# Reordered row loads, transposes and a weight load ahead of the first batch's last transform

## The chip, the cores and the metric

The kernel runs on one core of one Trainium2 chip. The metric is the device time of one execution in microseconds (us). Engines are named as in the profile: PE (TensorE, matmuls and transposes), DVE (VectorE), ACT (ScalarE), POOL (GpSimd) and SP (SyncE, which here only issues DMAs). DMAs issued by SP go through one queue (q1, hardware descriptors), DMAs issued by POOL through another (q0, software descriptors).

## The reference

The input `x` is 8 batches of 3136 rows by 256 channels, float32. Per batch and channel the rows are Fourier transformed, multiplied by a complex filter and transformed back; then a low-rank mix over the rows is added, and a two-layer perceptron over the channels.

```python
X = np.fft.rfft(x, axis=1)
Y = X * (filt_r + 1j * filt_i)
y = np.fft.irfft(Y, n=3136, axis=1)
u = y + (y^T @ U @ V)^T              # U: 3136x32, V: 32x3136
out = u + relu(u @ w_ch1) @ w_ch2    # w_ch1: 256x1024, w_ch2: 1024x256
```

## The kernel before

The 3136-point transform is split as 49 x 64. For one batch there are these stages, each a Python generator from which a hand-written order takes steps.

- `f1` / `f1_turned` (L241, L265): the 49-point transforms, a matmul with the table `ws` over four chunks `c` of `x`. `load_x` (L124) brings a chunk from float32 in DRAM to f16 in SBUF on POOL's queue.
- `mid` (L312): 64-point transform (`pz`, L374), product with the filter on DVE (`uv`, L382), inverse 64-point transform (`pe`, L338), copied by ACT to `e` (L348). There are 13 steps: pairs of frequencies, and the frequency 0 in a step of its own (the third, for batch 0). For batches 0 and 1 the input is turned on PE by `turn` (L289) instead of going through DRAM.
- The results are rearranged through DRAM. Every second pair is **stored** from `e` to `ct2` (L356, SP, 256 KB; batch 0 has five such stores, here store 1 to 5), and **row loads** (`load_e2`, L402, DMA at L406, SP) bring them to `eb`, in which partitions 32 to 95 hold the 48 frequencies' parts and the free dimension 64 rows of 256 channels. `load_e2(b, part, hs)` loads part 0, 1 or 2 (from stores 1-2, 3-4, 5) for row half 0, half 1 or both. In batch 0 the last two pairs go straight from `e` to `eb` without DRAM, by four small DMAs on SP and four on POOL (L352, 32 KB each).
- `rank` (L409): the low-rank part. `uh`, the transformed U, is multiplied with `e`; the result goes to `eb[0:32]` (L428, DVE).
- `s4` (L435): the last transform. Sixteen tiles `pu` of eight matmuls each (L446); the first eight need row half 0 of `eb`, the other eight row half 1. Batch 0 adds a matmul of constants to each tile (L443). DVE (L453) and ACT (L451) copy the tiles to `ut`.
- Then the main loop over 49 groups of 512 rows: `mm1` with `w1sb` (`phh`, L478, and ReLU on ACT, L481) and `mm2` with `w2sb` (`pc`, L501, L493, copied by DVE, L508). `plan` deals the steps of the later batches among the groups.

Ahead of the main loop everything of batch 0 runs in the order written from L532 on. Instructions of one engine run in program order, and a DMA that has to wait for an earlier one holds up all that its issuing engine has after it. PSUM tiles come from three tags of banks: `z` with 4, `m` and `o` with 2 each.

U is transformed first (`u_hat`, L210) into `tu`, which lies in `eb`. `u_ordered` (L224) copies part of it to `tp`, and `u_turned` (L227) makes 29 transposes on PE into two `z` banks and three copies on ACT to `uh`. `load_filters(i)` (L151, POOL's queue) loads the filters in three parts, and `spread_filters(i)` (L159) copies each part to partitions 64 to 127; for part 2 these are four copies on POOL. `w1sb` is loaded after them on POOL's queue (L538); `v_rows` (L201) is the POOL copy after that.

On POOL, `seen` (L563, L565) is a copy of a few elements of `eb`, which makes POOL wait until certain row loads have landed before it issues `load_x(1, 1)`, `load_x(1, 2)`, `load_x(1, 3)` and the load of `w2sb`.

Of the kernel before, what the change touches and what calls it, by code (L numbers as in the profile page):

```python
# [17 lines left out]
NK = 25  # L18
DM = 256
RANK = 32  # L20
# [59 lines left out]
def kernel(  # L80
# [37 lines left out]
    def view(t, off, dims):  # L118
        return bass.AP(tensor=t.tensor, offset=t.offset + off, ap=[[t.ap[0][0], t.shape[0]]] + [list(d) for d in dims])
# [39 lines left out]
    def spread_filters(i):  # L159
        s = slice(PARTS[i], PARTS[i + 1])  # L160
        copies = ((nc.vector.tensor_copy, nc.vector.tensor_copy), (nc.vector.tensor_copy, nc.scalar.copy),
                  (nc.gpsimd.tensor_copy, nc.gpsimd.tensor_copy))[i]

        for s in (slice(PARTS[2], 19), slice(19, NK)) if i == 2 else (s,):
            for f, copy in enumerate(copies):
                copy(fab[64:128, f, s, :], fab[0:64, f, s, :])


    a20 = [cst.tile([128, DM], F16, name=f"a20_{i}") for i in range(2)]
# [3 lines left out]
    uh = cst.tile([128, NK + 4, RANK], F16)  # L173
    nc.gpsimd.memset(uh[64:128, 0, :], 0)

    for i in range(3):
        load_filters(i)

    vnat = sb.tile([RANK, SEQ], F16, tag="ut", bufs=2, name="vnat")
    nc.gpsimd.dma_start(vnat, moe_V)  # L180
    w1sb = cst.tile([128, 2, NH], F16)
    w2sb = cst.tile([128, 8, DM], F16)

# [38 lines left out]
    tp = cst.tile([RANK, 4, 128], F16)  # L222

    def u_ordered():  # L224
        nc.scalar.copy(view(tp, 0, [[64, 8], [32, 2], [8, 4], [1, 8]]), view(tu, 128 * 20, [[64, 8], [8, 2], [16, 4], [1, 8]]))

    def u_turned():  # L227
        pt = bank("z", "put", F16)
        for k in range(NK):
            src = tu[:, 128 * k - 128:128 * k] if k else tu0  # L230
            m = 128 if k else NR
            nc.tensor.transpose(pt[0:m, RANK * k:RANK * k + RANK], src, idn[0:RANK, 0:RANK])
        pd = bank("z", "pd", F16)
        for k in range(4):
            nc.tensor.transpose(pd[:, RANK * k:RANK * k + RANK], tp[:, k, :], idn[0:RANK, 0:RANK])
        nc.scalar.copy(uh[:, 1:NK, :].rearrange("r k u -> r (k u)"), pt[:, RANK:RANK * NK])
        nc.scalar.copy(uh[0:NR, 0, :], pt[0:NR, 0:RANK])
        nc.scalar.copy(uh[:, NK:, :].rearrange("r k u -> r (k u)"), pd[:, 0:4 * RANK])


    def f1(b):  # L241
# [47 lines left out]
    def turn(b, g):  # L289
        if g == 3:  # L290
            t = a20[b]
            pt = bank("z", "pt", F16)
            for dh in range(2):
                nc.tensor.transpose(pt[0:64, 128 * dh:128 * dh + 128], t1[b][1][:, dh, :], idn)
            nc.scalar.copy(t[0:64], pt[0:64, 0:DM])
            return t
        t = sb.tile([128, 8, DM], F16, tag="a2", bufs=3, name="a2")
        for half in range(2):
            pt = bank("z" if b else ("m", "z")[half], "pt", F16)
            for i in range(4):  # L300
                for dh in range(2):
                    nc.tensor.transpose(pt[:, 256 * i + 128 * dh:256 * i + 128 * dh + 128],
                                        t1[b][0][:, dh, 8 * g + 4 * half + i, :], idn)
            (nc.scalar.copy if half or (g and b == 0) else nc.vector.tensor_copy)(  # L304
                t[:, 4 * half:4 * half + 4, :].rearrange("p k d -> p (k d)"), pt)
        return t
# [5 lines left out]
    def mid(b, tag="z"):  # L312
        a2 = {}

        def load_a2(g):
            if b < 2:
                a2[g] = turn(b, g)
                return
            if g == 3:
                t = a20[b % 2]  # L320
                nc.sync.dma_start(t[0:64], ct0[b].ap())
            else:
                t = sb.tile([128, 8, DM], F16, tag="a2", bufs=3, name="a2")
                nc.sync.dma_start(t, dram(ct1[b], 8 * g * DM, [[24 * DM, 128], [1, 8 * DM]]))
            a2[g] = t

        def s3(ks, uv, o):
            n = len(ks) * DM
            i = (ks[0] - 1) // 2
            pe = bank(tag, "pe")  # L330

            direct = b == 0 and ks[0] > 20
            ms = (gmp, gsmp) if direct or not ks[0] else (gm, gsm)
            if b == 0 and ks[0] > 8:

                nc.tensor.matmul(pe, m64[:, 0:128], m64[:, 0:512], start=True, stop=True, skip_group_check=True)
            for f, w in enumerate(ms if b == 0 else ms[:1]):
                nc.tensor.matmul(pe[:, 0:n], w, uv[:, f, o:o + n], start=(f == 0), stop=(b > 0 or f == 1))  # L338
            if not ks[0]:
                e3[b, 6] = sb.tile([128, DM], F16, tag="e30", bufs=2, name="e30")  # L340
                nc.scalar.copy(e3[b, 6], pe[:, 0:n])

                nc.sync.dma_start(eb[96:97, :, :], e3[b, 6][0:64])
                return
            if i % 2 == 0:
                e3[b, i // 2] = sb.tile([128, 4, DM], F16, tag="e3", bufs=6, name="e3")
            t = e3[b, i // 2]
            nc.scalar.copy(t[:, 2 * (i % 2):2 * (i % 2) + 2, :].rearrange("p k d -> p (k d)"), pe)  # L348
            if direct:
                for n, k in enumerate(ks):  # L350
                    for part in range(2):
                        (nc.sync if part else nc.gpsimd).dma_start(  # L352
                            eb[32 + row_of(k, part):33 + row_of(k, part), :, :],
                            t[64 * part:64 * part + 64, 2 * (i % 2) + n, :])
            elif i % 2:
                nc.sync.dma_start(dram(ct2[b][i // 4], 2 * (i % 4 - 1) * 128 * DM, [[DM, 128], [128 * DM, 4], [1, DM]]), t)  # L356

        if b == 0:
            spread_filters(0)
        for g in (0, 3, 1, 2) if b > 1 else (0, 3):  # L360
            load_a2(g)
        todo = []
        first_at = 2 if b < 2 else 6
        for i, ks in enumerate(PAIRS[:first_at] + [(0,)] + PAIRS[first_at:]):
            n = len(ks) * DM
            if b == 0 and i == 1:
                spread_filters(1)
            if b < 2 and i in (3, 7):
                load_a2(i // 4 + 1)
            pz = bank("z", "pz")  # L370
            if ks[0]:
                src = a2[(ks[0] - 1) // 8]
                k = (ks[0] - 1) % 8
                nc.tensor.matmul(pz, a2m, src[:, k:k + 2, :].rearrange("p k d -> p (k d)"), start=True, stop=True)  # L374
            else:
                nc.tensor.matmul(pz[:, 0:n], a20m, a2[3], start=True, stop=True)
            o = 512 if ks[0] % 4 == 3 else 0
            if o == 0:
                uv = sb.tile([128, 2, 1024], F16, tag="uv", bufs=4, name="uv")
            zin = bass.AP(tensor=pz.tensor, offset=pz.offset, ap=[[pz.ap[0][0], 128], [0, 2], [1, n]])  # L380
            fin = view(fab[:, 0, ks[0], 0:1], 0, [[NK * DM, 2], [1, n]])
            nc.vector.tensor_mul(uv[:, :, o:o + n], zin, fin)  # L382
            todo.append((ks, uv, o))
            if b and (o or not ks[0]):

                nc.vector.tensor_sub(uv[0:64, 0, 0:o + n], uv[0:64, 0, 0:o + n], uv[64:128, 1, 0:o + n])  # L386
                nc.vector.tensor_add(uv[64:128, 0, 0:o + n], uv[64:128, 0, 0:o + n], uv[0:64, 1, 0:o + n])  # L387
            if len(todo) > (3 if b else 2):
                s3(*todo.pop(0))
            yield  # L390
        for n, it in enumerate(todo):
            s3(*it)
            if b or n == 0:
                yield
        if b == 0:
            load_e2(0, 2, [0])
            load_e2(0, 1, [1])
            load_e2(0, 2, [1])
        yield


# [128 lines left out]
    s4s = [s4(b) for b in range(NB)]  # L530

    u_hat()  # L532
    for _ in f1s[0]:
        pass
    nc.gpsimd.dma_start(sv[32:97], sv_d.rearrange("k (r q) -> k r q", q=NQ))
    load_x(1, 0)
    spread_filters(2)
    nc.gpsimd.dma_start(w1sb, moe_w_ch1.rearrange("(h dd) c -> dd h c", h=2))  # L538
    v_rows(nc.gpsimd.tensor_copy, 0, 32)
    for i in range(13):  # L540
        next(mids[0])
        if i == 7:
            u_ordered()
        if i == 8:
            load_e2(0, 0)
            u_turned()
    load_e2(0, 1, [0])
    next(mids[0])
    next(ranks[0])
# [10 lines left out]
            next(f1s[1])  # L560
        nc.tensor.matmul(pw, m64[:, 0:128], m64[:, 0:512], start=(i == 0), stop=(i == 6))

    nc.gpsimd.tensor_copy(seen[64:66], eb[64:66, 8, 0:4])  # L563
    load_x(1, 1)
    nc.gpsimd.tensor_copy(seen[64:96], eb[64:96, 40, 0:4])  # L565
    for c in range(2, 4):
        load_x(1, c)
    nc.gpsimd.dma_start(w2sb, moe_w_ch2.rearrange("(t cc) e -> cc t e", t=8))
    for _ in s4s[0]:
        pass  # L570
# [60 lines left out]
```

## Time and profile before

| | us |
|---|---|
| runs of the kernel (3): median | 523.7 |
| lowest, highest | 521.31, 523.73 |
| profiled execution, its time | 523.45 |
| profiled execution, span of its instructions | 521.7 |
| PE busy | 497.5 (95% of the span) |
| ACT / DVE / POOL busy | 376.2 / 352.8 / 81.7 |
| mean granted PE clock | 0.984 |

The span runs from the first to the last instruction; times inside it are counted from its start. The page cuts the span into 40 slices of 13 us and gives, for each, the busy tenths of every engine and the granted PE clock in tenths of full speed. Other views list the instructions in order of time, the chain of waits that ended last, the busy time in chosen stretches, and the DMA queues in a stretch.

### The profile page before, as it was taken

The page shows a single profiled execution, that of the slowest core. Times are in us where ns is not written, and L with a number is a line of the kernel's source. Part 1 is how long each engine was busy: PE and PEld are TensorE (multiplying, and loading weights), DVE is VectorE, ACT ScalarE, POOL GpSimd, SP SyncE. Part 2 cuts the span into 40 slices and gives each one's busy share as a digit, 9 for nine tenths or more (in the row PEclk, how much of TensorE's full clock was granted, in tenths as well). Part 3 has the DMA queues.
Part 4 walks back from the last instruction along what each step waited for, and adds up shares of the span by engine and source line. Part 5 has one row for each costly group of instructions (what it writes and reads, how often), then busy time and mean ns, then how long its engine had stood idle before and what let it go on. Part 6 is the DMA issues. An engine that isn't in the chain of part 4 may idle for free.

```text
span 521.7 us, 11949 instructions
## 1 busy us (share of the span) xinstructions
PE 497.5 (95%) x4841; PEld 357.0 (68%) x4841; DVE 352.8 (68%) x470; ACT 376.2 (72%) x705; POOL 81.7 (16%) x121
## 2 busy tenths in 40 slices
PE   4794999999999999999999999999999999999997
PEld 4443666776777777777767777777677766776665
DVE  5885599589847987579747985689845995622122
ACT  6672778966996689767986689667985777666662
POOL 6672010002001111002101120002001010101110
PEclk9896799999999999999999999999999999999999
DMA  8995916966878297837877397828875136212213
GB/s 194 173 229 124 176 39 154 283 218 149 208 222 265 66 186 198 292 137 163 219 230 249 70 189 217 286 99 191 233 232 204 62 127 200 100 44 83 80 41 122
DMA packets 67287, 88.09 MB, mean 169 GB/s; under 512 B 4875, under 2 KB 51787, under 8 KB 67232
## 3 DMA queue, kind: packets, MB, share of 16 engines
q0 software_dynamic: 14768, 41.65, 32.6%
q1 hardware_dynamic: 52464, 45.68, 28.9%
q8 instruction: 38, 0.62, 0.5%
q14 instruction: 17, 0.14, 0.1%
HBM read 55.07 MB, written 47.64 MB: 197 GB/s over the span
## 4 chain that ended last, share of the span: by engine, by line
PE 85%; DVE 3%; DMA 1%; ACT 1%; SPq 1%; issue 0%
PE pc L501 32%; PE phh L478 32%; PE pu L446 5%; PE pc L493 4%; PE pf L250 4%; PE pe L338 3%; PE pz L374 3%; DVE uv L382 2%; DMA eb<-ct 1%; PE ph L413 1%; ACT h L481 0%; DVE uv L386 0%; DVE uv L387 0%; DVE och L508 0%; SPq L352 0%; DVE a L304 0%
## 5 line engine op out<-in xcount | busy, mean ns | idle before, releaser
L481 ACT ACTIVATE h<-phh 128x512 f16<-128x512 f32 x392 | 236.5, 605 | 87.7 <-PE phh L478 86.6
L478 PE MATMUL phh<-ut,w1sb 128*128 128x512 f16 (+7 forms) x896 | 234.3, 353 | 0.4 <-DVE ut L453 0.2
L501 PE MATMUL pc<-w2sb,h 128*128 128x256 f16 x1568 | 234.2, 272 | 0.0
L501 PEld LDWEIGHTS <-h 128*128 128x128 f16 x1568 | 151.5, 97 | 90.4
L508 DVE COPY och<-pc 128x512 f32<-128x512 f32 x98 | 67.6, 690 | 99.6 <-PE pc L493 98.4
L382 DVE TENSOR_TENSOR uv<-pz,fab 128x1024 f16<-128x1024 f32 (+1 forms) x104 | 120.9, 1179 | 13.4 <-PE pz L374 11.9
L513 POOL DMA_DIRECT2D out_dram<-och x48 | 39.1, 814 | 402.7 <-DVE och L508 395.1
L478 PEld LDWEIGHTS <-w1sb 128*128 128x128 f16 x896 | 77.9, 98 | 19.7 <-issue 2.2
L348 ACT CAST e<-pe 128x512 f16<-128x512 f32 x96 | 56.7, 591 | 19.3 <-PE pe L338 18.4
L453 DVE CAST ut<-pu 128x392 f16<-128x392 f32 x92 | 48.9, 559 | 24.6 <-PE pu L446 21.0
L255 ACT CAST asb<-pf 98x512 f16<-98x512 f32 x96 | 57.3, 600 | 0.2
L493 PE MATMUL pc<-idn,ut 128*128 128x128 f16 (+1 forms) x400 | 54.0, 219 | 0.0
L446 PE MATMUL pu<-sv,eb 97*128 97x49 f16 x1024 | 41.9, 189 | 6.8 <-DMA eb<-ct 6.8
L428 DVE COPY eb<-h 32x4096 f16<-32x4096 f16 x32 | 38.2, 1232 | 14.2 <-ACT h L425 14.2
L446 PEld LDWEIGHTS <-eb 97*128 97x128 f16 x1024 | 38.9, 99 | 8.0 <-issue 7.2
L338 PE MATMUL pe<-uv,m 128*128 128x512 f16 (+1 forms) x117 | 41.3, 371 | 2.0 <-ACT e L348 1.0
L493 PEld LDWEIGHTS <-ut 128*128 128x128 f16 (+1 forms) x400 | 38.2, 98 | 5.2 <-issue 0.8
L374 PE MATMUL pz<-a,m 128*128 128x512 f16 x96 | 36.6, 384 | 1.4 <-DVE a L304 1.0
L250 PE MATMUL pf<-x,ws 98*98 98x256 f16 x192 | 36.6, 273 | 0.0
L386 DVE TENSOR_TENSOR uv<-uv 64x1024 f16<-64x1024 f16 (+1 forms) x49 | 30.9, 630 | 1.7
L387 DVE TENSOR_TENSOR uv<-uv 64x1024 f16<-64x1024 f16 (+1 forms) x49 | 30.7, 627 | 0.7
L250 PEld LDWEIGHTS <-ws 98*98 98x98 f16 x192 | 22.4, 125 | 9.1 <-issue 0.4
(81 smaller groups left out, 226.2 us busy)
## 6 DMA issues: line engine op xcount, KB each, us to landing
out_dram<-och POOLq DMA_DIRECT2D x48, 512.0 KB, 3.9
ct<-e SPq DMA_DIRECT2D x47, 256.0 KB
eb<-ct SPq DMA_DIRECT2D x46, 256.0 KB
x<-in_x_dram POOLq DMA_DIRECT2D x28, 392.0 KB, 6.7
ct<-asb SPq DMA_DIRECT2D x24, 384.0 KB
a<-ct SPq DMA_DIRECT2D x18, 512.0 KB
x<-in_x_dram POOLq DMA_DIRECT2D x4, 384.0 KB, 8.0
ws<-ws SPq DMA_DIRECT2D x1, 600.2 KB
```

Source lines behind the costliest of these rows:

```text
L250: nc.tensor.matmul(pf[0:98, 256 * s:256 * s + 256], ws[:, (8 * c + j) * 98:(8 * c + j + 1) * 98], t[:, j, :], start=(s == 0), stop=True, s ...
L255: nc.scalar.copy(dst, src)
L338: nc.tensor.matmul(pe[:, 0:n], w, uv[:, f, o:o + n], start=(f == 0), stop=(b > 0 or f == 1))
L348: nc.scalar.copy(t[:, 2 * (i % 2):2 * (i % 2) + 2, :].rearrange("p k d -> p (k d)"), pe)
L374: nc.tensor.matmul(pz, a2m, src[:, k:k + 2, :].rearrange("p k d -> p (k d)"), start=True, stop=True)
L382: nc.vector.tensor_mul(uv[:, :, o:o + n], zin, fin)
L446: nc.tensor.matmul(pu[:, NQ * i:NQ * i + NQ], eb[:, 8 * n + i, d], sv[:, 8 * g + i, :], start=(i == 0), stop=True, skip_group_check=True)
L478: nc.tensor.matmul(ph[:, o:o + n], w1sb[:, dh, 128 * t:128 * t + 128], utv(b)[:, dh, t0:t0 + n], start=(dh == 0), stop=(dh == 1), skip_gro ...
L481: nc.scalar.activation(h, ph, RELU)
L493: nc.tensor.matmul(d, w, idn, start=False, stop=(dh == 1), skip_group_check=True)
L501: nc.tensor.matmul(o, gr.h[tt][:, 128 * i:128 * i + 128], w2sb[:, tt, :], start=(tt == 0), stop=False, skip_group_check=True)
L508: nc.vector.tensor_copy(gr.och[:, i - 1:i + 1, :], gr.pc.rearrange("p (j d) -> p j d", d=DM))
```

## The change

Six edits, all ahead of the main loop.

1. `load_filters(1)`, `load_filters(2)` and the load of `vnat` stand after `u_hat()` in the program, and `u_ordered()` is put ahead of them, as a POOL copy instead of an ACT copy.
2. The 29 transposes of U stand ahead of the steps of `x`'s last chunk in `f1_turned(0)`, in one bank of tag `m` instead of two of tag `z`; the copies to `uh` stay after step 8 of `mid` (steps are counted from 0) and are two instead of three.
3. In `turn`, batch 0's tiles take other tags of banks.
4. The load of `w1sb` stands between the two pairs of POOL copies of filter part 2 instead of after both.
5. Part 0's row loads: before, both halves were issued after step 8 (after store 3, ahead of store 4). Now half 0 is issued after step 10 (after store 4), and half 1 together with half 1 of parts 1 and 2, after all loads of half 0.
6. `seen` copies from partitions 32 to 63 and 64 to 95, of half 0 ahead of `load_x(1, 1)` and of half 1 ahead of `load_x(1, 2)`; before, ahead of `load_x(1, 1)` it read two partitions alone.

```diff
     def spread_filters(i):
...
             for f, copy in enumerate(copies):
                 copy(fab[64:128, f, s, :], fab[0:64, f, s, :])
+            yield
...
-    for i in range(3):
-        load_filters(i)
+    load_filters(0)
     vnat = sb.tile([RANK, SEQ], F16, tag="ut", bufs=2, name="vnat")
-    nc.gpsimd.dma_start(vnat, moe_V)
...
     def u_ordered():
-        nc.scalar.copy(view(tp, ...), view(tu, 128 * 20, ...))
+        nc.gpsimd.tensor_copy(view(tp, ...), view(tu, 128 * 20, ...))
     def u_turned():
-        pt = bank("z", "put", F16)
+        pt = bank("m", "put", F16)
...
-        pd = bank("z", "pd", F16)
         for k in range(4):
-            nc.tensor.transpose(pd[:, RANK * k:RANK * k + RANK], tp[:, k, :], idn[0:RANK, 0:RANK])
-        nc.scalar.copy(uh[:, 1:NK, :]..., pt[:, RANK:RANK * NK])
+            nc.tensor.transpose(pt[:, RANK * (NK + k):RANK * (NK + k + 1)], tp[:, k, :], idn[0:RANK, 0:RANK])
+        return pt
+    def u_copied(pt):
+        nc.scalar.copy(uh[:, 1:, :]..., pt[:, RANK:RANK * (NK + 4)])
         nc.scalar.copy(uh[0:NR, 0, :], pt[0:NR, 0:RANK])
-        nc.scalar.copy(uh[:, NK:, :]..., pd[:, 0:4 * RANK])
...
     def turn(b, g):
-            pt = bank("z", "pt", F16)
+            pt = bank("z" if b else "o", "pt", F16)
...
-            pt = bank("z" if b else ("m", "z")[half], "pt", F16)
+            pt = bank("m" if b == 0 and g == 1 and half == 0 else "z", "pt", F16)
...
         if b == 0:
             load_e2(0, 2, [0])
-            load_e2(0, 1, [1])
-            load_e2(0, 2, [1])
+            for part in range(3):
+                load_e2(0, part, [1])
...
     u_hat()
-    for _ in f1s[0]:
-        pass
+    u_ordered()
+    for i in range(1, 3):
+        load_filters(i)
+    nc.gpsimd.dma_start(vnat, moe_V)
+    for i in range(16):
+        if i == 12:
+            put = u_turned()
+        next(f1s[0])
     nc.gpsimd.dma_start(sv[32:97], ...)
     load_x(1, 0)
-    spread_filters(2)
+    late = spread_filters(2)
+    next(late)
     nc.gpsimd.dma_start(w1sb, ...)
+    next(late)
     v_rows(nc.gpsimd.tensor_copy, 0, 32)
     for i in range(13):
         next(mids[0])
-        if i == 7:
-            u_ordered()
         if i == 8:
-            load_e2(0, 0)
-            u_turned()
+            u_copied(put)
+        if i == 10:
+            load_e2(0, 0, [0])
     load_e2(0, 1, [0])
...
-    nc.gpsimd.tensor_copy(seen[64:66], eb[64:66, 8, 0:4])
-    load_x(1, 1)
-    nc.gpsimd.tensor_copy(seen[64:96], eb[64:96, 40, 0:4])
-    for c in range(2, 4):
-        load_x(1, c)
+    for h in range(2):
+        for p in (32, 64):
+            nc.gpsimd.tensor_copy(seen[p:p + 32], eb[p:p + 32, 8 + 32 * h, 0:4])
+        for c in ((1,), (2, 3))[h]:
+            load_x(1, c)
     nc.gpsimd.dma_start(w2sb, ...)
```

## The prediction

> **What bounds it now.** I read the page first: PE is busy 95% of the span, and the low digits stand in the first five slices alone, with the granted clock low in the fourth and fifth (39 to 65 us). All six edits lie there. Behind it PE is the bound; a main loop that starts earlier ends earlier by the same time.
>
> ```profile
> PE   4794999999999999999999999999999999999997
> ...
> PEclk9896799999999999999999999999999999999999
> ```
>
> Then I took the chain of waits from 36 to 60 us and the instructions of SP and of PE in order of time (columns: start, length, what).
>
> ```profile
> 42.37 0.59 SPq L352
> ...
> 43.90 0.58 SPq L406
> 44.48 0.04 issue
> 44.52 6.65 DMA eb<-ct
> 51.17 0.14 issue
> 51.30 0.49 PE pu L446 x8
> ```
>
> ```profile
> 27.91 3.63 SPq L356 DMA_DIRECT2D ct<-e  x2
> 31.91 1.22 SPq L406 DMA_DIRECT2D eb<-ct  x2
> 33.47 2.09 SPq L356 DMA_DIRECT2D ct<-e  x2
> 39.89 0.52 SPq L406 DMA_DIRECT2D eb<-ct  x1
> 40.50 2.46 SPq L352 DMA_DIRECT2D eb<-e  x4
> 43.06 2.15 SPq L406 DMA_DIRECT2D eb<-ct  x3
> ```
>
> ```profile
> 46.59 0.49 PE L446 MATMUL pu<-sv,eb 97*128 97x49 f16 x8 [5.68 <-DMA eb<-ct]
> ...
> 51.30 0.49 PE L446 MATMUL pu<-sv,eb 97*128 97x49 f16 x8 [1.09 <-DMA eb<-ct]
> ```
>
> The reader is to see two waits of PE for row loads: 5.68 us ahead of half 0, 1.09 us ahead of half 1. SP issues stores 2 and 3 at 27.91 and 31.18, stores 4 and 5 at 33.47 and 35.20, and then sits until 39.89: part 1's load waits for store 4, which the trace's semaphore records have landing at 39.87, 6.4 us after its issue (store 3: 6.7). Behind that wait stand the four direct DMAs and the last loads. From store 4's landing to the first `pu` are 6.7 us: 0.57 for the load's issue, 2.56 for four direct DMAs, 3.0 from the issue of part 2's half 0 at 43.06 to its landing at 46.07, and 0.5 until PE runs.
>
> Why does a store take 6.4 us? Two stretches of the DMA view (queue: packets, MB, share of the engines' time):
>
> ```profile
> q0 software_dynamic: 202, 0.41, 91.5%
> ```
>
> ```profile
> q1 hardware_dynamic: 1513, 1.20, 103.8%
> q0 software_dynamic: 19, 0.02, 3.7%
> ```
>
> The first is 31.5 to 34.5 us, the second 35.0 to 38.5. In the first, `w1sb` (POOL's queue, issued at 29.97) moves 0.41 MB and SP's queue has no packet at all, although two stores and two loads are issued by then. When `w1sb` is through, SP's queue moves 1.20 MB in 3.5 us (343 GB/s): stores 3, 4, 5 and the two early loads, in that order.
>
> **The change part by part.**
>
> *`w1sb` earlier (edit 4).* It goes ahead of two POOL copies of 1.46 us: issued at about 27.1 instead of 29.97. POOL's queue is then still busy with a chunk of `x`, whose packets end near 29, so `w1sb` runs from about 28.9 to 32.6 (0.51 MB at 0.41 MB per 3.0 us). The price: stores 1 and 2 (25.99, 27.91), which before used the gap from 28.5 to 31, now stand behind it. The two copies end 0.74 us later (its issue), near 30.8; the first product that needs them is the eleventh, not before 31.9. That cover is 1 us; were it gone, DVE would wait the difference.
>
> *U's transposes earlier (edits 1 to 3).* At 29.81 PE spends 1.11 us on them between steps of `mid` (29.81 to 30.92). Now they run while PE waits for the last chunk (14.46 to 15.54, 1.07 us): cost 0 to 0.1. DVE's products are back to back from 21.95 to 28.3 and from 28.46 to 30.8, then wait 0.53 for `pz` behind the transposes; that goes, the last product ends 0.5 earlier. ACT loses `u_ordered` (0.6, just ahead of store 3's second copy) and one copy of U (0.25, against 0.1 for the longer first one): store 3 goes 0.5 earlier, store 4 0.95, to about 32.5, store 5 0.8. What is late next is ACT's chain of `e`, the U copies still in it. `u_ordered` as a POOL copy has no row; bounds are 0.5 (512 elements at the 1.46 us per 1536 of L166) and 1.0 (at the 2.91 us per 1568 of the strided L202). I take 1.0: it starts near 12.5, where POOL waits until 13.31 anyway, and the filter loads behind it wait for `x` again at 15.54, which absorbs the rest. The banks: `put` holds one `m` bank from 14.5 to step 8; in that time `m` serves the last chunk's second tile and one tile of `turn`, whose bank ACT or DVE has emptied by 17.3. Cost 0.
>
> *Half 0 first (edit 5).* Ahead of store 4 in SP's queue now stand no loads. In order after `w1sb` (32.6): store 1, the DMA of frequency 0, stores 2, 3, 4: 1.08 MB at 343 GB/s is 3.1 us, so store 4's packets end at 35.7. Before, they ended near 38.1 by the same reckoning (35.0 and four transfers of 0.262 MB), 15 of its 16 parts landed at 38.68 and the last at 39.87; a tail of 0.6 to 1.8, of which I take 1.1: landing 36.8 (bounds: 34.8, with the 2.3 us of the quiet store at 84.42; 38.9, with the old 6.4). Half 0 of part 0 needs stores 1 and 2 and can hold SP to about 35, not beyond store 4's landing. Then the same 6.7 us: **first `pu` at 43.5 instead of 46.59, 3.1 us earlier** (bounds 41.5 and 45.6).
>
> *Half 1 and the chunks of `x` (edits 5, 6).* SP issues half 1's three loads right behind, to about 42.5; at 3.0 to 4.4 us to landing (the rows at 43.06 and 43.90) they are in by 47. PE needs 3.5 us for half 0, to 47.0. `load_x(1, 1)` now waits for all of half 0: landing 43.0 and 1.0 us as between 48.31 and 49.35, issue 44.0 (before 44.17), packets 2.3 us later (before: 44.17 to 46.5), at 46.3, so it no longer holds up half 1, whose last load took 6.65 us before. The wait of 1.1 goes. Chunks 2, 3 and `w2sb` follow half 1's landing: about 48 instead of 49.35; chunk 3 then lands near 55, needed near 55.6, and `w2sb` near 58 (8.9 us after its issue before), needed near 58.4. That cover is thin, and half a microsecond late would cost as much.
>
> *Clock.* Granted clock by windows (columns: window, its length, PE, PEld, DVE, ACT and POOL busy, PEclk, DMA share, GB/s):
>
> ```profile
> 13.40:16.80 3.40, 1.96 (x38) 1.65 (x35) 2.42 (x9) 2.22 (x10) 2.28 (x5) 1.00 1.15 172
> 16.80:20.20 3.40, 3.23 (x20) 1.94 (x20) 2.42 (x6) 1.28 (x4) 3.37 (x6) 0.50 1.00 138
> ...
> 50.90:54.30 3.40, 3.00 (x64) 3.03 (x65) 1.70 (x3) 1.27 (x3) 0.98 (x2) 0.50 0.81 150
> 54.30:57.70 3.40, 3.18 (x25) 1.79 (x22) 0.66 (x2) 2.02 (x5) 0.00 (x0) 0.50 1.21 184
> ```
>
> The clock changes at steps of 3.41 us in the trace's clock records. PE idle for 1.4 of 3.4 us halves it in the next step; it stays 0.50 to 57.76, since the wait at 50.2 breaks the dense stretch. After the change `pu` runs without a gap, so one dense step fits and the clock returns near 48 to 50. A tile takes 0.43 at half clock; at full clock DVE's 0.57 for every second tile sets 0.29. Some four tiles gain 0.14 each, and the first ReLU comes 0.4 earlier (four `phh` take 1.87 where 0.43 per pair is the later rate): 1.0 us (bounds 0 and 2.4).
>
> **Sum.** 3.1 + 1.1 + 1.0 = 5.2 us off the profiled execution's 523.45 (span 521.7 and 1.75 around it): **518.3**. The profiled time stands 0.25 under the median, so nothing is corrected for that.
>
> [...]
>
> **Rivals.**
> - *The wait moves to stores 1 and 2.* Held behind `w1sb`, they land late, SP stands at half 0 of part 0, and store 5 and all behind it follow. For it: no store got through beside `w1sb`. Against: the queue needs only 1.6 us for both once `w1sb` is through. If SP stood there until 37, part 2's half 0 would end the wait, `pu` would start near 45.2: 1.4 earlier, with the 1.1 of half 1 and no clock, 521.0. Chance 0.14.
> - *Slower: half 1 falls behind `load_x(1, 1)`.* If SP reaches half 1's three loads after the chunk's packets start (over 4 us later than I put it), 0.64 MB wait for the chunk's 4 us of packets: in by 52, `pu` ends near 55.5 instead of 54.8, and chunk 3 and `w2sb`, now behind half 1, come 3 us late. That is 1 to 3 slower: 525.5. For it: the load issued at 44.52 landed at 51.17. Against: half 0's landing now gates the chunk. Chance 0.06.
> - *The clock does not fall.* The idle stretch shrinks to some 3 us over two steps. Then the tiles run at 0.29 from the start, 2.4 us less for sixteen, and the main loop starts 0.5 faster: 3.1 + 1.1 + 2.9 = 7.1, 516.3. Chance 0.08, as the row at 13.40 speaks against it.
>
> **Numbers.** My forecast has 0.72. The range reaches from 516.2, just under the clock rival, to 521.8, over the first rival, and leaves the slower one and the ends of the unknown tail out. About 0.5%, 2.6 us, is what can be told from no change: faster than 521.1 holds my forecast, the clock rival and a small part of the first: 0.81; within it 0.13; slower 0.06.
>
> **What would show it.** SP: store 4 at 32.5, landing before 38; the direct DMAs from about 37.4. PE: first `pu` between 42 and 45, no wait of 1 us ahead of the ninth tile. q0 with packets from 29 to 32.6, then q1 alone. PEclk back at 1.00 before 51. First `phh` near 50 instead of 55.05. Wrong: store 4 landing after 39, a new wait of SP ahead of part 0's load that lasts beyond 36, PE waiting for chunk 3 or `w2sb`, or DVE for the filter copies near 32.

## The result, and the profile after

| | before | changed |
|---|---|---|
| median of 9 runs each, us | 523.6 (519.62 to 523.73) | 518.92 (517.33 to 521.4) |
| ratio to before, with 95% interval | 1 | 0.9932 (0.9903 to 0.9961) |
| profiled execution, us | 523.45 | 517.65 |
| its span, us | 521.7 | 515.9 |
| first `pu`, ninth `pu`, first `phh`, first `pc` | 46.59, 51.30, 55.05, 63.05 | 43.90, 46.50, 49.94, 57.24 |

The change is faster by 0.7% by the ratio, which here is that of the means (519.05 to 522.60); the medians differ by 4.7 us, or 0.9%. A time of 518.3 was forecast. Line numbers of `seen` and of the loads at the end of POOL's list differ by some ten between the two kernels; those of the rows below are the same.

The page of the changed kernel, the two rows shown of before:

```profile
PE   4787999999999999999999999999999999999997
...
PEclk9898999999999999999999999999999999999999
```

PE's fourth slice has gone from 4 to 7 tenths, and the granted clock of the fourth and fifth from 6 and 7 to 8 and 9. (In the third, PE has gone from 9 to 8.) The instructions of SP in order of time (start, length, what):

```profile
27.95 5.03 SPq L356 DMA_DIRECT2D ct<-e  x3
35.58 0.59 SPq L406 DMA_DIRECT2D eb<-ct  x1
36.27 0.53 SPq L356 DMA_DIRECT2D ct<-e  x1
37.08 0.53 SPq L406 DMA_DIRECT2D eb<-ct  x1
37.66 2.52 SPq L352 DMA_DIRECT2D eb<-e  x4
40.23 3.23 SPq L406 DMA_DIRECT2D eb<-ct  x4
```

Stores 2, 3 and 4 leave at 27.95, 30.76 and 32.62. Then SP stands until 35.58 for part 0's load, since store 2 lands at 35.49 by the semaphore records (31.82 before: `w1sb`, which lands at 35.00, is now in its way). Store 5 waits behind it, from the end of its copy near 34.7 to 36.27. Store 4 lands at 37.00, 2.9 us sooner than before, and the rest follows. PE, with what ended its waits:

```profile
43.90 0.36 PE L446 MATMUL pu<-sv,eb 97*128 97x49 f16 x8 [3.27 <-DMA eb<-ct]
...
54.54 0.35 PE L278 MATMUL pf<-ws,x 98*128 98x98 f16 x4 [0.17 <-DMA x<-in_x_dram]
...
57.24 0.60 PE L501 MATMUL pc<-w2sb,h 128*128 128x256 f16 x4 [0.23 <-DMA w2sb<-in_moe_w_ch_dram]
```

The 5.68 us ahead of half 0 are 3.27; the wait ahead of half 1 is gone. Two new short waits stand where the cover was said to be thin, for chunk 3 and for `w2sb`, and the chain of waits now runs through `w2sb`'s load:

```profile
37.08 5.67 DMA eb<-ct
42.77 3.48 DMA eb<-ct
...
48.41 8.79 DMA w2sb<-in_moe_w_ch_dram
57.20 0.04 issue
57.24 0.60 PE pc L501 x4
```

The clock, by windows (columns as in the prediction; PEclk is the third from the end):

```profile
45.20:48.60 3.40, 3.40 (x77) 3.40 (x73) 2.71 (x6) 2.05 (x5) 1.62 (x5) 0.50 0.84 141
48.60:52.00 3.40, 3.01 (x54) 2.20 (x51) 1.73 (x4) 2.67 (x8) 1.26 (x2) 1.00 0.91 155
```

One step at half clock instead of four. **What makes the time:** from the first `pc` to the end of the span are 458.65 us before (521.7 - 63.05) and 458.66 after (515.9 - 57.24), and 458.6 to 458.7 in all but two of the experiments below (458.9 and 459.3 there). All that this change can move lies ahead of the first `pc`, so the start of `pc` in a profile stands for its time. The same kernel spreads by some 4 us from run to run (more in some of the experiments), and two profiles of the changed kernel have the first `pc` at 57.24 and 59.51, so single profiles are read for mechanisms and the ratios for sizes.

### The profile page after: what moved, and what is told of

It is laid out like the page before. It is cut to its first block, busy times and chain, and to the rows that moved or that the text cites. A ratio compares the mean times of both kernels' runs of the same rounds, so it can differ in the third digit from the quotient of the medians.

```text
span 515.9 us, 11950 instructions
## 1 busy us (share of the span) xinstructions
PE 494.3 (96%) x4841; PEld 354.1 (69%) x4841; DVE 352.3 (68%) x470; ACT 375.0 (73%) x703; POOL 82.4 (16%) x124
## 4 chain that ended last, share of the span: by engine, by line
PE 86%; DMA 7%; DVE 4%; ACT 2%; issue 1%; POOL 0%; POOLq 0%; SPq 0%
PE pc L501 32%; PE phh L478 31%; PE pu L446 5%; PE pf L250 4%; PE pc L493 4%; PE pe L338 4%; PE pz L374 4%; DMA eb<-ct 2%; DVE uv L382 2%; DMA w2sb<-in_moe_w_ch_dram 2%; DMA x<-in_x_dram 2%; DMA usb<-in_moe_U_dram 1%; PE ph L413 1%; DMA ct<-e 1%; ACT a L304 1%; ACT e L348 1%
## 5 line engine op out<-in xcount | busy, mean ns | idle before, releaser
L453 DVE CAST ut<-pu 128x392 f16<-128x392 f32 x92 | 48.6, 559 | 20.0 <-PE pu L446 18.6
L446 PE MATMUL pu<-sv,eb 97*128 97x49 f16 x1024 | 40.5, 187 | 3.3 <-DMA eb<-ct 3.3
L446 PEld LDWEIGHTS <-eb 97*128 97x128 f16 x1024 | 37.6, 98 | 4.4 <-DVE eb L428 3.6
```

The source lines that it names most:

```text
L446: nc.tensor.matmul(pu[:, NQ * i:NQ * i + NQ], eb[:, 8 * n + i, d], sv[:, 8 * g + i, :], start=(i == 0), stop=True, skip_group_check=True)
```

## The experiments

Ratios are to the kernel before on the same chip, with 95% intervals; "changed" has 0.9932 (0.9903 to 0.9961).

| kernel | median us | ratio | first `pu`, first `pc` in its profile |
|---|---|---|---|
| changed, again | 518.93 | 0.9933 (0.9909 to 0.9957) | 45.31, 59.51 |
| changed without edit 4 | 519.27 | 0.9932 (0.9902 to 0.9961) | 45.54, 59.08 |
| changed without edit 5 | 521.98 | 0.9989 (0.9953 to 1.0025) | 48.35, 62.38 |
| changed without edit 6 | 519.8 | 0.9941 (0.9907 to 0.9974) | 43.41, 58.23 |
| changed without edits 1 to 3 | 518.82 | 0.9928 (0.9899 to 0.9958) | 46.33, 64.37 (a late execution) |
| before with edit 5 | 522.15 | 1.0021 (0.9995 to 1.0047) | 44.64, 61.06 |
| before with edits 5 and 6 | 520.39 | 0.9963 (0.9946 to 0.9981) | 45.29, 60.95 |
| changed, `w1sb` away | 518.91 (one run) | | 41.20, 58.51 |
| changed, PE kept busy | 520.29 | 0.998 (0.996 to 1.0001) | 43.57, 58.24 |
| changed, `sv` late | 518.86 | 0.995 (0.9933 to 0.9968) | 44.86, 58.83 |
| changed, `sv` on SP | 519.42 | 0.995 (0.9928 to 0.9971) | 45.56, 60.84 |
| changed, chunk 1 early, PE kept busy | 520.52 | 0.9965 (0.994 to 0.9989) | 46.12, 59.07 |

### One edit taken back at a time

**Edit 4**, `w1sb` behind the four copies again:

```diff
     next(late)
-    nc.gpsimd.dma_start(w1sb, ...)
     next(late)
+    nc.gpsimd.dma_start(w1sb, ...)
```

> The changed kernel with the load of w1sb put back behind all four filter copies. My theory (software-queue transfers shut out SP's queue, so w1sb's place decides which stores are late): w1sb's packets run 31.5 to 35.0 us again, stores 1 and 2 land by 32 as before, stores 3 and 4 wait for w1sb; store 4 lands at 37.2 to 38.4 instead of 37.0 and the first pu starts at 44.0 to 45.1 instead of 43.9: 0.1 to 1.2 us longer. Rival A (w1sb's place is the gain): first pu at 46, some 2.5 us longer. Rival B (queues share the engines, its place does not matter): stores 3 and 4 land as in the changed kernel, first pu at 43.9.

Measured: `w1sb` issued at 30.05, stores 1 and 2 in at 30.91 and 31.77, stores 3 and 4 at 36.52 and 37.28. Store 4 lands 0.3 us later than in the changed kernel, and the ratio is the same to the last digit. What `w1sb` shuts out on one side of store 2 it lets through on the other. Its first `pu`, at 45.54, is later than I expected, but the changed kernel's other profile has 45.31. Rival A is refuted; rival B, for the total, can't be told from my theory by this run.

**Edit 5**, both halves of part 0 ahead of store 4 again:

```diff
         if i == 8:
+            load_e2(0, 0)
             u_copied(put)
-        if i == 10:
-            load_e2(0, 0, [0])
```

> The changed kernel with part 0's row loads, both halves, back after step 8, ahead of store 4. My theory: with w1sb early, store 2 lands only at 35.5, SP stands at part 0's loads until then, so store 4 is issued near 36.8 instead of 32.6 and lands near 40; the first pu starts at 46.5 to 47.5 and the kernel is 2 to 4 us slower than the changed one, no better than the kernel before. Rival A (edits 4 and 6 are worth their gain without edit 5): first pu at 44.5, under 1 us slower than the changed one.

SP in order of time:

```profile
26.94 3.17 SPq L356 DMA_DIRECT2D ct<-e  x2
35.05 1.22 SPq L406 DMA_DIRECT2D eb<-ct  x2
36.37 1.08 SPq L356 DMA_DIRECT2D ct<-e  x2
41.73 0.52 SPq L406 DMA_DIRECT2D eb<-ct  x1
```

Store 2 lands at 34.96, part 0's loads wait for it, and store 4, whose data were ready long before, leaves at 36.37 and lands at 41.72. The first `pu` starts at 48.35, and the gain over the kernel before is within its interval of nothing. That is my theory; but store 4 landed 1.7 us later than I put it, and the first `pu` came 0.9 us after the end of my range.

**Edit 6**, the old `seen`:

```diff
-    for h in range(2):
-        for p in (32, 64):
-            nc.gpsimd.tensor_copy(seen[p:p + 32], eb[p:p + 32, 8 + 32 * h, 0:4])
-        for c in ((1,), (2, 3))[h]:
-            load_x(1, c)
+    nc.gpsimd.tensor_copy(seen[64:66], eb[64:66, 8, 0:4])
+    load_x(1, 1)
+    nc.gpsimd.tensor_copy(seen[64:96], eb[64:96, 40, 0:4])
+    for c in range(2, 4):
+        load_x(1, c)
```

> The changed kernel with the old seen copies, so that load_x(1,1) waits for two partitions of half 0 only. My theory: it is issued near 43.2 instead of 44.25, its packets start near 44.5, and the last of half 1's rows are shut out until they are through: they land near 48 to 50 instead of 46.24, PE waits 1 to 3 us ahead of the ninth pu, and the kernel is 0.5 to 2.5 us slower. Rival (half 1's rows are through by then, or the queues share): they land by 46.5, no wait, and chunks 2, 3 and w2sb come 1 us sooner, so 0 to 0.4 us faster.

My theory did not come true. The chunk left at 42.82, half 1's last load at 42.23 landed at 46.76, and PE did not wait for it (ninth `pu` at 46.90). The rival's picture holds: with SP as early as this, half 1 is ahead of the chunk without the new `seen`. The ratio is inside the changed kernel's interval. Only `w2sb` did not come sooner (58.19).

**Edits 1 to 3**, U as before (the place of the filter loads, which is part of edit 1, stays as in the changed kernel):

```diff
-    u_ordered()
     for i in range(1, 3):
...
-        if i == 12:
-            put = u_turned()
...
+        if i == 7:
+            u_ordered()
         if i == 8:
-            u_copied(put)
+            u_turned()
```

> The changed kernel without edits 1 to 3: U ordered on ACT and turned at step 8 in two z banks. My theory: store 4 is issued near 33.5 instead of 32.6, DVE's last product ends 0.5 later, and since store 2's landing (35.5) and not store 4's issue holds SP here, the first pu starts only 0 to 0.9 us later: 0 to 0.9 us slower. Rival (the transposes are the larger part of the gain): first pu 2 us later, 2 us slower.

0.9928: nothing lost, the low end of what I expected; the rival's 2 us are refuted by the ratio. Its profiled execution is the slowest of its eleven runs (524.78 us, 6 above the median): there store 2 landed only at 36.98 and the first `pu` started at 46.33, 2.4 us behind the changed kernel's. So the mechanism that I expected is not shown by it, and only the ratio speaks.

### Edit 5 alone, and with edit 6

```diff
         if i == 8:
-            load_e2(0, 0)
             u_turned()
+        if i == 10:
+            load_e2(0, 0, [0])
...
-            load_e2(0, 1, [1])
-            load_e2(0, 2, [1])
+            for part in range(3):
+                load_e2(0, part, [1])
```

> The kernel before with edit 5 alone (row loads of half 0 first, none ahead of store 4). My theory as the runs so far leave it (the order of SP's queue is the gain, U's transposes and w1sb's place hardly matter): store 4 issued at 33.5, landing 37 to 38.4, first pu 44 to 45.5 instead of 46.59; load_x(1,1) issued near 43.5, so half 1's last rows may be held up for 1 to 3 us; 1.5 to 3 us faster than the kernel before. Rival (edit 5 needs w1sb early): first pu at 46, no more than 0.5 us faster.

PE in its profile, and the DMA queues from 46.5 to 49.5 us:

```profile
44.64 0.49 PE L446 MATMUL pu<-sv,eb 97*128 97x49 f16 x8 [4.00 <-DMA eb<-ct]
...
50.48 0.36 PE L446 MATMUL pu<-sv,eb 97*128 97x49 f16 x8 [2.29 <-DMA eb<-ct]
```

```profile
q0 software_dynamic: 92, 0.34, 57.4%
q1 hardware_dynamic: 46, 0.15, 13.2%
```

Half 0 comes 2 us sooner, as I expected, and half 1 gives it back: its last load, issued at 43.53 just behind `load_x(1, 1)` (43.38), lands at 50.34, after 6.8 us. The time did not fall (1.0021). I had the mechanism and the wrong price: the held-up rows take all. (The first `pc` of this one profile is 2 us ahead of that of before, 61.06 against 63.05, but on this chip the kernel before has a median of 521.77, which by the constant above is a first `pc` near 61.4.) With edit 6 added (the same `seen` loop as in the changed kernel):

> The kernel before with edits 5 and 6 alone. My theory (edit 5 brings half 0 forward, and it counts only when half 1 is kept from load_x(1,1), which edit 6 does): first pu at 44 to 45.5, no wait of PE over 0.5 us ahead of the ninth tile, first pc near 59, 0.992 to 0.997 of the kernel before. Rival (without w1sb early the pair gains nothing, as edit 5 alone did): 0.998 or more.

No wait ahead of the ninth tile (48.71, right behind the eighth), half 1's last row in at 48.29 with the chunk issued at 46.03. The ratio 0.9963 is inside what I expected; `pc`, at 60.95 and not near 59, waits 0.87 us for `w2sb`. So the order of SP's queue is worth its time only when half 1 is kept from the chunk, by edit 6 or by being earlier itself, as the run without edit 6 had it. By the ratios about half of the change's gain is in edits 5 and 6. That edits 1 to 4 add the rest is barely clear of the intervals (0.9963, 0.9946 to 0.9981, against 0.9932, 0.9903 to 0.9961), and how it divides between edits 1 to 3 and edit 4, each of which can be missed alone, is open.

### Is it `w1sb` that holds the stores?

```diff
     next(late)
-    nc.gpsimd.dma_start(w1sb, ...)
     next(late)
...
             load_x(1, c)
+        if not h:
+            nc.gpsimd.dma_start(w1sb, ...)
```

> The changed kernel with the load of w1sb moved behind load_x(1,1), so that no transfer of POOL's queue runs between 30 and 36 us. It measures the shutting out by itself; the main loop then has to wait for w1sb. My theory: stores 2, 3 and 4 land within 2.3 to 3.6 us of their issue (in the changed kernel 7.5, 5.6, 4.4), part 0's load is issued right after store 4 (33 to 34 instead of 35.58), the first pu starts at 41.8 to 42.8 instead of 43.9; first phh only near 53, when w1sb is in; 2 to 3 us slower. Rival (stores are slow for another reason, the queues share): landings as in the changed kernel within 1 us, first pu 43.5 to 44.

The queues from 31.5 to 34.5 us, the stretch in which the kernel before has no packet of q1, then SP and PE:

```profile
q1 hardware_dynamic: 706, 0.49, 62.1%
```

```profile
26.73 5.02 SPq L356 DMA_DIRECT2D ct<-e  x3
32.14 0.59 SPq L406 DMA_DIRECT2D eb<-ct  x1
33.49 0.36 SPq L356 DMA_DIRECT2D ct<-e  x1
33.97 0.53 SPq L406 DMA_DIRECT2D eb<-ct  x1
```

```profile
41.20 0.36 PE L446 MATMUL pu<-sv,eb 97*128 97x49 f16 x8 [1.80 <-DMA eb<-ct]
```

With no transfer of POOL's queue about, store 4 lands 2.26 us after its issue (31.40 to 33.66; 4.38 in the changed kernel) and store 3 after 3.26; store 2, issued while the chunk of `x` still runs, takes 5.33, which I had put at 3.6 at most. The first `pu` starts at 41.20, 2.7 us ahead of the changed kernel. So the shutting out is shown. The first `phh` then waits for `w1sb` until 50.23, and the one run took 518.91: the 2 to 3 us that I expected to lose are not seen. Its first `pc`, at 58.51, lies between those of the two profiles of the changed kernel; one run says no more.

### Is it the clock that sets the end?

```diff
     pw = bank("o", "pw")
-    for i in range(7):
+    for i in range(22):
...
-    nc.tensor.matmul(pw, ..., start=(i == 0), stop=(i == 6))
+    nc.tensor.matmul(pw, ..., start=(i == 0), stop=(i == 21))
```

> The changed kernel with 22 instead of 7 matmuls of constants between the rank part and the first pu, so that PE is busy until about 43.6 us instead of 40.5. My theory: the granted clock stays at 1.00, the sixteen pu tiles take 4.3 to 4.7 us instead of 5.5, first phh 1 us earlier; but first pc waits for w2sb, which lands when it did (57.2), and PE waits 1 us for chunk 3, so the kernel gains only 0 to 0.4 us. Rival (the clock sets the end): 1 us or more faster.

The window from the first to the last tile, and the first `pc`:

```profile
43.50:47.70 4.20, 4.13 (x143) 4.16 (x144) 3.27 (x7) 3.23 (x7) 2.26 (x7) 1.00 0.67 124
```

```profile
58.24 0.60 PE L501 MATMUL pc<-w2sb,h 128*128 128x256 f16 x4 [0.80 <-DMA w2sb<-in_moe_w_ch_dram]
```

The clock stays at 1.00, sixteen tiles take 4.2 us, the first `phh` starts at 48.36, 1.6 sooner than in the changed kernel, and it is of no use: PE waits 1.11 us for chunk 3 and 0.80 for `w2sb`, which lands at 58.20. There is no gain, and the rival is refuted. But the ratio is not just equal, as I expected: it is 0.998 against 0.9932, with intervals that only just touch, and the profiled execution is the fastest of its ten. Why it is slower is not settled.

### Three tries at the new bound

First, `sv` out of the way of `w1sb`, into the stretch in which the engines idle (`dma_start(sv[32:97], ...)` moved behind `v_rows`):

> The changed kernel with the load of the table sv (0.4 MB on POOL's queue, needed at the first pu) issued after the POOL copy v_rows near 33.6 instead of at 20.2. The DMA engines idle from 34.7 to 37.0 in the changed kernel, and the queue ahead of w1sb becomes 1.3 us shorter. My theory: w1sb's packets end near 31.2, store 2 lands near 34.2, store 5 is no longer held up, sv's packets run in the idle stretch, first pu at 42.3 to 43.2, w2sb lands about 1 us earlier, and as first pc is bound by it the kernel is 0.5 to 1.3 us faster than the changed one. Rival (sv shuts out the loads of half 0 in turn): first pu at 44 to 45, 0 to 1 us slower.

Half of it came (though the stretch does not idle: SP's queue has 29% of the engines' time in 34.7 to 37.0 of the changed kernel): store 2 in at 30.85, part 0's load at 32.40, store 4 in at 35.68. But `sv`, issued at 34.66, landed only at 41.86, and POOL's four direct DMAs behind it at 43.1 to 44.2 instead of 40.2 to 43.1, so the first `pu` started at 44.86. The rival is right. Then the same table on SP's queue after store 4 (`nc.sync.dma_start(sv[32:97], ...)` ahead of `load_e2(0, 0, [0])`):

> The changed kernel with the table sv loaded on SP's queue after store 4 instead of on POOL's queue ahead of load_x(1,0). My theory: w1sb's packets end 1.3 us earlier, store 2 lands near 34.2 instead of 35.5, part 0's load and store 5 go 1 us earlier, sv runs while the engines idle, first pu at 42.6 to 43.4 and w2sb lands 0.5 to 1.2 us earlier: 0.5 to 1.2 us faster than the changed kernel. Rival (sv ahead of half 0's rows in SP's queue delays them): first pu at 44 or later, no gain.

Again the early part came (part 0's load at 33.27, store 4 in at 36.15), and then store 5, issued at 33.97, landed at 41.90 and held part 2's load; first `pu` at 45.56. (The profiled execution, 521.97, is the slowest of its eleven.) The rival is right. And chunk 1 early, with PE kept busy:

```diff
     v_rows(nc.gpsimd.tensor_copy, 0, 32)
+    load_x(1, 1)
...
-        for c in ((1,), (2, 3))[h]:
-            load_x(1, c)
+        if h == 0:
+            load_x(1, 2)
+    load_x(1, 3)
```

> The changed kernel with load_x(1,1) issued after the POOL copy v_rows (near 33.6 us, into the stretch in which the DMA engines idle), load_x(1,2) after half 0's rows, and 22 matmuls of constants ahead of the first pu. My theory (first pc is bound by what POOL's queue still has to move after half 0): the chunk shuts out the loads of half 0 for 2 us, first pu at 44 to 45.5, but w2sb lands 1 to 2.5 us earlier, first pc at 55.5 to 57, 0.5 to 2 us faster than the changed kernel. Rival (what is shut out costs as much as it saves): first pu at 46 or later, no gain.

The chunk ran from 34.41 to 41.71, store 5 landed at 42.84, the first `pu` started at 46.12, and `w2sb` came at 58.47. No gain: the rival is right. What the three may have in common is in the last section. The changed kernel once more, beside these on one chip:

> The changed kernel itself, unaltered, beside the others on one chip. My theory: the time is the start of the first pc plus a constant 460.4 us, and the first pc is bound by w2sb's landing, so 0.991 to 0.996 of the kernel before. Rival (the first measurement was lucky): 0.996 or more.

0.9933: the gain is confirmed. Its store 4 landed at 37.28, the first `pu` started at 45.31 and the clock was low for two steps (45.0 to 51.8), with `phh` at 52.52. Here `pc` came 7.0 us after `phh`, with `w2sb` in just before (59.47).

## Why the prediction was right, and where not

- **Store 4 earlier.** Issue 32.5 and landing 36.8 forecast; 32.62 and 37.00 in the profile. That `w1sb` shuts the stores out is shown by the run without it (store 4 in after 2.26 us, not 4.38). But the working from `w1sb`'s end to the landing did not hold, and the landing is right by luck. The working put 1.08 MB behind `w1sb`, from 32.6 to 35.7 at 343 GB/s, and a tail of 1.1 us. In the profile store 1 and the DMA of frequency 0 got through ahead of `w1sb` (they landed at 30.74 and 30.95), so less was left; but it went at half the rate. The queues of the changed kernel from 32.0 to 36.75 us:

```profile
q1 hardware_dynamic: 1559, 0.77, 55.9%
q0 software_dynamic: 71, 0.11, 14.1%
```

That is 162 GB/s. Nine of store 4's sixteen parts had landed at 34.93, the last at 37.00: the parts came sooner than forecast and the tail was twice as long. `w1sb`'s last packets ran among them, to near 34.5; that they made the tail is not shown.
- **First `pu` at 43.5.** 43.90 in one profile, 45.31 in the other. The step that fell short is "then the same 6.7 us": it took 6.9 and 8.0. Part 1's load needed 5.67 and 6.55 us to land instead of 4.0, with store 5 and POOL's direct DMAs now beside it; no run takes these away by themselves. A part of the first rival is in here too: store 5 left 1.6 us late behind the wait for store 2.
- **Half 1.** No wait ahead of the ninth tile, as forecast. That edit 6 is what does it is only half true: it is needed with edit 5 alone (1.0021 against 0.9963), and not needed beside the other edits (0.9941).
- **U's transposes, 0.5 us.** They freed DVE and PE: DVE's last product ended at 35.69 instead of 35.97, 0.3 of the 0.5, and store 4 was issued 0.85 us earlier. The ratio shows nothing of it (0.9928 without these edits). A likely reason, argued and not shown, is that store 4's landing followed what was ahead of it in the queues and not its issue, and that SP stood until 35.5 for store 2 in any case.
- **Clock, 1.0 us (0 to 2.4).** Five tiles ran before the clock fell, and it came back after one step: sixteen tiles took 5.46 us from the first to the last start against 8.02, of which 1.1 is the wait and 1.5 the clock; 0.7 more came between `phh` and `pc`. So the term was 2.0 in this pair, twice the forecast. In the second profile two steps were low and 1.2 was left for this term. How the steps lie to the tiles differs between the two profiles (the clock falls at 45.2 with the first `pu` at 43.90, at 45.0 with it at 45.31), so a part of it is chance; and the run with PE kept busy shows that what the clock gives beyond this is cut off by `w2sb`.
- **The sum.** Forecast 3.1 + 1.1 + 1.0 = 5.2. In the profiled pair 2.7 + 1.1 + 2.0 = 5.8 (523.45 to 517.65). With the second profile of the changed kernel it is 1.28 + 1.09 + 1.17 = 3.54. Over all runs it is 3.6 us by the ratio (2.0 to 5.1): the profiled execution of before lies 0.85 above the mean of its kernel and that of the changed kernel 1.4 below. So 5.2 was too much by nearly half of what was measured and lies just above the interval; that the forecast of 518.3 came within 0.7 us of the median is in part luck, as it was taken off an execution above the mean. By the second profile, the part that was too much is half 0's, 1.3 instead of 3.1.
- **The thin cover** of chunk 3 and `w2sb` was named and priced at "half a microsecond"; it is the bound of the changed kernel's profile, 0.17 and 0.23 us here and up to 1.11 (chunk 3) and 0.87 (`w2sb`) in the experiments. So one sign of being wrong, PE waiting for chunk 3 or `w2sb`, did come, in small. I had not counted it in the sum.
- **Rivals.** The slower one did not come in the changed kernel: the chunk's packets start near 45.5, half 1 is in at 46.24. It is real, though: edit 5 alone met it (50.34). The clock rival did not come by itself, and when forced gave no time.

## What to carry to other kernels

Before a long transfer or a wait is moved, write down for each queue what is ahead of it and behind it: here one load that waited for a late store held four others that did not need it, and one transfer of the other queue decided which store was late. An edit that looks sound can be worth nothing alone, as edit 5 here, when a second wait stands right behind the one that it removes; take edits back one at a time and put them in one at a time. And find the one event from which the rest of the run is constant (here the first `pc`): it tells at once which of two gains will be seen.

## What the runs showed of the hardware

- In the kernel before, the load of `w1sb` on the software queue left SP's queue nothing from 31.5 to 34.5 us: 0.41 MB of `w1sb` and no packet of q1 in 3.0 us, where the same 3.0 us without it carry 0.49 MB of q1; store 4 takes 2.26 us without it instead of 6.40 in the kernel before and 4.38 in the changed one. In the changed kernel, from 30.0 to 32.0 us, q1 has 8.6% beside `w1sb`, most of it in the first half microsecond. Beside a chunk of `x` on the same queue q1 got more: in the changed kernel q1 has 14.4% of the engines' time from 27.0 to 28.5 us, beside `sv` and a chunk, and in the kernel with edit 5 alone 13.2% beside a chunk (shown above). That is about the time of two of the sixteen engines.
- In the kernel with `sv` on SP the eight direct DMAs of 32 KB, each into one partition, lie together with other transfers, and the queues move little. From 39.5 to 41.0 us:

```profile
q1 hardware_dynamic: 173, 0.07, 74.3%
q0 software_dynamic: 16, 0.01, 9.7%
```

0.08 MB in 1.5 us at 84% busy engines, where q1 elsewhere moves 1.20 MB in 3.5 us. In the changed kernel POOL's four take 4.1 to 4.8 us to land, in the kernel before 2.8 to 4.5. The view does not say whose packets these are: store 5, which landed at 41.90, may have a share. The packet records of the trace have q1's packets of 512 bytes at 118 ns each there, and at 31 ns from 41 to 44 us in the kernel before, where POOL's four had landed. The last three tries met such a stretch (POOL's four took 6.3 to 7.4 us to land with `sv` late, 6.1 to 7.0 with `sv` on SP, 5.2 to 6.2 with chunk 1 early). That it is the pile that made half 0 late, and whether the single partition or the size of the packets makes it slow, was not tried.
- In these profiles the granted clock fell after steps of 3.4 us in which PE was idle for only a part. Before, 5.68 us idle up to 46.59 gave 0.50 from 44.1 to 57.8; in the changed kernel 3.27 us idle, spread over two steps (2.1 us of it in the step from 41.8 to 45.2), still gave 0.50 from 45.2 to 48.6; with 1.80 us idle (`w1sb` away; at most 1.3 us of it in one step) it stayed at 1.00.
